# Moving a product behind stores, a load ahead of a fetch, and dealing a vector engine's rows anew, in a kernel of RWKV-7 attention and a SoLU layer

## The chip, the cores and the metric

The kernel runs on one core of a Trainium2 chip. The metric is device time in microseconds of one execution, and the median of several executions is compared. The core has five engines that run their own instruction streams in order and meet at semaphores: PE (TensorE, matrix products and transposes into the PSUM banks), DVE (VectorE), ACT (ScalarE), POOL (GpSimd) and SP (SyncE, which here only issues DMAs). POOL and ACT issue DMAs too.

## What is computed

The first part is a linear recurrence. For each of 4 batches and 8 heads a 40 x 40 state is carried over 768 steps; y is read before the state is updated. The second part takes y as 3072 rows of 320 numbers through a layer with 1024 hidden units.

```python
for t in range(S):
    y[:, :, t] = einsum('bhd,bhde->bhe', r_t, state)
    Sa = einsum('bhde,bhe->bhd', state, a_t)
    state = state * w_t[:, :, None, :] - einsum('bhd,bhe->bhde', Sa, b_t) + einsum('bhd,bhe->bhde', v_t, k_t)
x = y.transpose(0, 2, 1, 3).reshape(B * S, H * D)
h = x @ w_in
sm = softmax(h)                                  # over the 1024 hidden units
solu = h * sm
ln = (solu - mean(solu)) / sqrt(var(solu) + 1e-6) * g_ln
out = ln @ w_out
```

w_in and w_out arrive as 64-bit floats, and the kernel makes 32-bit floats of them itself, mostly with integer operations.

## The kernel before

**Chunks.** 64 steps of two batches are a chunk; a tile has 128 partitions, 64 for each batch. 12 chunks in time by 2 pairs of batches give 24 chunks, numbered 0 to 23, two in turn being independent of each other. Within a chunk the recurrence becomes matrix products: the decay's running sums (log of w, a product with a triangle on PE named pcum, exponentials ei and inv), a and b scaled by them (aT, bT; kb holds b and k times inv, made by POOL, L371), the matrix N of all pairs of a and b (nt, L453, "norm"), and the inverse of a triangular system that N gives.

**The inverse.** N of a chunk is stored to DRAM (four DMAs of nt_dram, L461). When two chunks are there, which make a block (GRP = 2; block n holds chunks 2n and 2n + 1), it is fetched back with another layout (blk, L470), and DVE solves all 32 systems of the block in step: 30 inverse steps, each of which adds to the columns found so far a multiple of a row of N (L486, or L494 and L497 in two halves). A first part (L480, L481) sets the tile up and belongs to step 1. After step 30 the result is stored (uu_dram, L503, SP) and brought back per chunk as tu and uh (L516, L518). tu is turned by DVE (flip, L524) and completed by PE, ACT, PE, ACT ("couple", "close"; py, wy, tu).

**Passes.** The main loop has passes i = -1 to 26. Pass i works on chunk i's solution (PE pu, then lu: masked on DVE, L422, and copied by ACT, L656), on chunk i + 1's scores (PE ps; DVE makes psi and lv out of it, L422; then PE px, which uses the bank pair of ps), on chunk i + 5's front (a and b turned on PE, aT on DVE, L405; norm, L453), on chunk i - 2's hidden layer (PE h, DVE nmax L735, ACT exp L743, DVE e L751, ACT sq L764, POOL rs L766), and on chunk i - 3's output (PE plnT L777, ACT lnT, PE po). PE's pst turns the carried state; DVE's tot, st and x (L682 to L698) end pass i's recurrence, and x goes through DRAM to the hidden layer. The kernel begins with a prologue that makes the fronts of chunks 0 to 4; -6 to -3 are its four turns and -2 its end.

**PSUM.** There are eight banks, used as four pairs named A, B, C and h. A new tile of a pair waits until the tile before it in that pair has been read. C holds in turn a front's turned tiles, pu, the shared tile of norm, couple and close (py), and pcum; h is used by the prologue's pcum, then by the hidden layer from pass 2 on.

**Orders.** The order on each engine is the program's, written out by hand. The inverse steps and the making of 32-bit weights are dealt out by a table `plans`: a row for each of -6 to 5 (the prologue's have five places between its steps, or two), and two rows, 24 and 25, for even and odd passes from 6 on. A pass from -1 on has six places: [0] after the front's aT and ahead of lu, [1] between lu and psi, [2] after the load of v, ahead of nmax, [3] after exp and ahead of tot, [4] after tot, [5] after st and x. In a row a number is so many inverse steps of the oldest open block ("o": of blocks that the pass needs finished, only), and b, s, f are the three parts of a weight tile's conversion: b two DVE operations (L192, L193), s three of ACT (L195, L196, L199 or L202), f three of DVE (L204 to L206); f also issues POOL's next weight load (L181) where one follows. There are 5 tiles of w_in and 8 of w_out.

**Queues.** SP issues the loads of w, b, a, k, v (L307), the fetches of tu and uh, the stores of the inverse, x's way back and the output. In the built program a DMA on SP also waits for the landing of the eighth before it. POOL issues, in its own order among the products of L371, N's stores, blk's fetch, loads of r and most loads of w_out (L181), and x's stores.

Around the change the program reads, in pass i with j = i + 5: `scaled(j + 1)` (b's and k's product), `norm(j)` (N and its stores), and in odd j `begin_inverse` (two memsets, blk's fetch). In the prologue's end: `bring(0)`, `bring(1)` (the fetches), then `load_keys(5, "bak")`.

Of the kernel before, what the change touches and what calls it, by code (L numbers as in the profile page):

```python
# [18 lines left out]
C = 64  # L19
# [4 lines left out]
LAG = 2  # L24
# [28 lines left out]
def kernel(  # L53
# [18 lines left out]
    nc = tc.nc  # L72
# [400 lines left out]
    def invert(n):  # L473
# [7 lines left out]
        nc.vector.memset(flat[0:C, 0::Q + 2], 1.0)  # L481
        for j in range(1, Q - 1):
            m, n_c = Q - 1 - j, (j + 1) // 2
            if n_c < 3:
                for c in range(n_c):
                    nc.vector.scalar_tensor_tensor(out=u[:, c, j + 1:Q], in0=nb[:, j, j + 1:Q], scalar=u[:, c, j:j + 1],  # L486
                                                   in1=u[:, c, j + 1:Q], op0=ALU.mult, op1=ALU.add)
            else:
                parts_ = ((0, n_c // 2), (n_c // 2, n_c))
                ts = []  # L490
                for lo, hi in parts_:
                    prod = two.tile([P, 72], FP32, tag="prod", name="prod")
                    ts.append(prod[:, 0:(hi - lo) * m].rearrange("p (c r) -> p c r", c=hi - lo))
                    nc.vector.tensor_tensor(out=ts[-1], in0=nb[:, j:j + 1, j + 1:Q].to_broadcast([P, hi - lo, m]),  # L494
                                            in1=u[:, lo:hi, j:j + 1].to_broadcast([P, hi - lo, m]), op=ALU.mult)
                for x, (lo, hi) in zip(ts, parts_):
                    nc.vector.tensor_tensor(out=u[:, lo:hi, j + 1:Q], in0=u[:, lo:hi, j + 1:Q], in1=x, op=ALU.add)  # L497
            if j < Q - 2:
                yield
# [143 lines left out]
    def solved(i):  # L643

        if not ok(i):
            return lambda: None
        d = st[i]
        t = pair("C", "pu")
        for u in in_turn(lambda p, q, g, h: (p ^ h, p)):
            p, q, g, h = u  # L650
            at, x = (2 * q + g) * W2, half(p ^ h)
            mm(t[half(p), h, at:at + W2], d["tu"][x, 4 * p + 2 * q + g, Q:], x0[x, h, 2 * q + g])
        lu = d["lu"] = two.tile([P, H, W2], FP32, tag="lu", name="lu", bufs=1)
        o, y = lu.rearrange("p (j h) c -> p h j c", h=2), t[:, :, 0:4 * W2].rearrange("p h (j d) -> p h j d", j=4)
        masked(o[:, :, :, 0:C], y[:, :, :, 0:C])
        return lambda: nc.scalar.copy(out=o[:, :, :, C:], in_=y[:, :, :, C:])  # L656

    def read(i, part):
        if not ok(i):
# [169 lines left out]
    for n in range(2):  # L829
# [4 lines left out]
    decay_turned(0)()  # L834
    plans = {
# [14 lines left out]
    }  # L850
# [42 lines left out]
    begin_inverse(1)  # L893
    scaled(2, "k")
    scaled(3, "k")
    load_keys(6, "w")
    vector(plan[1])
    decay(5)()
    logged(6)
    load_values(1)  # L900
    load_r(1)
    scaled(4, "k")
    bring(0)
    bring(1)
    load_keys(5, "bak")
    load_keys(7, "w")
    land(3, nc.sync)

# [1 line left out]
    for i in range(-1, N + LAG + 1):  # L910
# [58 lines left out]
        scores(i + 1)()  # L969
        flip(i + 1)  # L970
        run(2)
        scaled(j + 1)
        stated_r(i + 1)
        run(3)
        norm(j)
        if ok(j) and j % GRP == GRP - 1:
            begin_inverse(j // GRP)
        by_value(i + 2)
        run(4)
        if i == LAG + 1:  # L980
# [71 lines left out]
```

## Time and profile before

| what | value |
|---|---|
| time, median of three executions | 552.5 us (551.71, 552.5, 558.36) |
| the profiled execution | 558.81 us, of which span 557.0 us |
| granted clock of PE in it, mean | 0.969 |
| PE busy | 489.3 us, 88% of the span |
| DVE busy | 447.1 us, 80% |
| ACT busy | 300.7 us, 54% |
| POOL busy | 216.3 us, 39% |

The profile is of one execution, and its numbers are set against its own span. A row of a timeline gives the start, the length, the engine, the line of the program, the operation, the tile written and those read, the shape, how often, and in square brackets the idle time just before it with what released it. Rows of SP (SPq) are DMA issues. The chain of waits is followed back from the last instruction: each piece is what the next one waited for. Busy times overlap between engines, and an idle engine costs nothing where another sets the end.

### The profile page before, as it was taken

To read this page: it belongs to the slowest core of one execution; us is meant where nothing else is said; L and a number is where in the kernel's file an instruction comes from. 1 tells how busy PE (TensorE), PEld (TensorE's weight loads), DVE (VectorE), ACT (ScalarE), POOL (GpSimd) and SP (SyncE) were. 2 spreads that over 40 slices of the span, in tenths; PEclk is the share of its full clock that TensorE was granted. 3 is DMA by queue.
4 is the path that set the end of the run, shared out by engine and by line. 5 is a ranking of instruction groups with operands and counts; after the bars stand their busy time and mean duration, and the time that the engine had idled before them with its cause. 6 is when DMAs were issued, how large, how long until landed. Compare 5 with 4: busy or idle time off the path is not lost.

```text
span 557.0 us, 28207 instructions
## 1 busy us (share of the span) xinstructions
PE 489.3 (88%) x12081; PEld 401.1 (72%) x12081; DVE 447.1 (80%) x1801; ACT 300.7 (54%) x584; POOL 216.3 (39%) x368
## 2 busy tenths in 40 slices
PE   4644763878999999999999999999999999999996
PEld 3434653755788778878887887788778877787666
DVE  4598984799888998998989989989989788544432
ACT  4625473388376556565655655566555544653332
POOL 4456335264254264355435452644452502110110
PEclk9999976698999999999999999999999999999999
DMA  8997887665546666467566466566643432410120
GB/s 151 153 160 143 171 137 185 137 142 103 111 95 124 135 126 135 96 136 154 105 139 146 110 132 122 124 127 123 137 107 73 107 90 71 90 37 27 49 60 25
DMA packets 198157, 63.98 MB, mean 115 GB/s; under 512 B 170904, under 2 KB 190336, under 8 KB 198032
## 3 DMA queue, kind: packets, MB, share of 16 engines
q1 hardware_dynamic: 185296, 42.22, 39.8%
q0 software_dynamic: 10384, 19.30, 13.9%
q8 instruction: 95, 1.56, 1.2%
q10 hardware_dynamic: 2352, 0.66, 0.7%
q14 instruction: 30, 0.25, 0.1%
HBM read 47.96 MB, written 14.16 MB: 112 GB/s over the span
## 4 chain that ended last, share of the span: by engine, by line
PE 62%; DVE 13%; issue 9%; DMA 7%; ACT 3%; SPq 3%; POOL 2%; ACTq 0%; DVEq 0%; POOLq 0%
PE h L281 15%; PE po L281 14%; PE px L281 7%; PE py L281 5%; PE pyo L281 5%; PE pcum L281 3%; PE pu L281 3%; PE ps L281 2%; SPq L307 2%; DVE uu L497 2%; DVE prod L494 2%; PE plnT L777 2%; DMA raw_w<-in_w_dram 1%; PE pa L378 1%; PE psr L281 1%
## 5 line engine op out<-in xcount | busy, mean ns | idle before, releaser
L281 PE MATMUL h<-w_in,xT 64*64 64x512 f32 (+1 forms) x1164 | 123.1, 521 | 2.3 <-ACT lnT L786 1.1
L497 DVE TENSOR_TENSOR uu<-uu,prod 128x60 f32<-128x60 f32 (+21 forms) x624 | 117.0, 227 | 0.0
L281 PE MATMUL po<-w,lnT 128*128 128x160 f32 x768 | 109.3, 300 | 2.4 <-ACT x L641 1.6
L281 PEld LDWEIGHTS po<-w,lnT 128*128 128x128 f32 x768 | 105.3, 190 | 4.7 <-ACT x L641 2.8
L494 DVE TENSOR_TENSOR prod<-blk,uu 128x60 f32<-128x60 f32 (+21 forms) x624 | 107.1, 211 | 1.6
L766 POOL TENSOR_TENSOR rs<-var,mhalf 128x1 f32<-128x1 f32 x24 | 13.9, 578 | 182.7 <-ACT var L765 161.2
L461 POOL DMA_DIRECT2D nt_dram<-nt x86 | 50.8, 597 | 66.7 <-ACT nt L453 65.3
L281 PEld LDWEIGHTS h<-w_in,xT 64*64 64x64 f32 x1164 | 37.7, 134 | 22.2 <-issue 17.6
L735 DVE TENSOR_REDUCE nmax<-h 128x1 f32<-128x1024 f32 x24 | 29.3, 1220 | 23.7 <-PE h L281 23.7
L281 PE MATMUL pcum<-lw,cst 128*128 128x160 f32 x96 | 24.9, 394 | 16.2 <-ACT lw L347 16.2
L764 ACT ACTIVATE sq<-e,mu 128x1024 f32<-128x1024 f32 x24 | 26.9, 1119 | 16.6 <-DVE e L751 16.6
L307 POOL DMA_DIRECT2D raw_r<-in_r_dram x48 | 34.0, 714 | 1.2 <-issue 1.2
L751 DVE SCALAR_TENSOR_TENSOR e<-h,e 128x1024 f32<-128x1024 f32 x24 | 29.4, 1223 | 6.1 <-ACT e L743 6.1
L536 ACT ACTIVATE wy<-py,cst 128x256 f32<-128x256 f32 x24 | 11.3, 472 | 41.9 <-PE py L281 41.9
L743 ACT ACTIVATE e<-h,nmax 128x1024 f32<-128x1024 f32 x24 | 26.6, 1110 | 13.2 <-DVE nmax L735 13.1
L371 POOL TENSOR_TENSOR kb<-raw_b,inv 128x320 f32<-128x320 f32 x24 | 21.1, 878 | 31.2 <-DMA raw_b<-in_b_dram 23.9
L281 PEld LDWEIGHTS pcum<-lw,cst 128*128 128x128 f32 x96 | 17.8, 239 | 19.8 <-ACT lw L347 16.8
L281 PE MATMUL px<-st,aT 40*64 40x128 f32 x704 | 25.1, 281 | 6.0 <-DVE lv L422 5.0
L388 ACT COPY rT<-pb 104x512 f32<-104x512 f32 x24 | 14.1, 586 | 29.5 <-PE pb L378 29.5
L281 PEld LDWEIGHTS py<-aT,bT 40*64 40x64 f32 x768 | 17.0, 156 | 17.0 <-ACT lu L656 8.5
L801 DVE TENSOR_SCALAR osb<-po,rs 128x320 f32<-128x320 f32 x21 | 11.6, 551 | 21.7 <-POOL rs L766 12.9
L682 DVE TENSOR_TENSOR tot<-pyo,st 104x512 f32<-104x512 f32 (+1 forms) x44 | 23.9, 584 | 6.2 <-PE pyo L281 5.9
(145 smaller groups left out, 1099.4 us busy)
## 6 DMA issues: line engine op xcount, KB each, us to landing
xT<-x_dram SPq DMA_DIRECT2D x48, 160.0 KB, 3.6
blk<-nt_dram POOLq DMA_DIRECT2D x22, 256.0 KB, 4.0
raw_w<-in_w_dram SPq DMA_DIRECT2D x48, 80.0 KB, 3.5
a<-in_a_dram SPq DMA_DIRECT2D x48, 80.0 KB, 3.8
raw_r<-in_r_dram POOLq DMA_DIRECT2D x48, 80.0 KB, 3.4
lv<-in_v_dram SPq DMA_DIRECT2D x48, 80.0 KB, 3.1
out_dram<-osb SPq DMA_DIRECT2D x47, 80.0 KB, 2.6
raw_b<-in_b_dram SPq DMA_DIRECT2D x44, 80.0 KB, 3.6
```

Of the source, the lines that this page charges most:

```text
L281: nc.tensor.matmul(o, lhsT=lhsT, rhs=rhs, start=start, stop=stop, skip_group_check=True)
L307: queue.dma_start(out=x[half(p), :, 0:D], in_=ap[2 * bp + p, :, ci * C:(ci + 1) * C, :].rearrange("h t d -> t h d"))
L371: nc.gpsimd.tensor_tensor(out=kb[:, j:j + H, 0:D], in0=d["raw_" + n], in1=heads(d["inv"]), op=ALU.mult)
L388: nc.scalar.copy(out=o[0:W2], in_=t)
L461: queue.dma_start(out=blocks[n][e].rearrange("(a x h) s c -> a x s h c", a=GRP, x=2)[at, x], in_=nt[home:home + Q].rearrange("p h j c -> p ...
L494: nc.vector.tensor_tensor(out=ts[-1], in0=nb[:, j:j + 1, j + 1:Q].to_broadcast([P, hi - lo, m]), in1=u[:, lo:hi, j:j + 1].to_broadcast([P, ...
L497: nc.vector.tensor_tensor(out=u[:, lo:hi, j + 1:Q], in0=u[:, lo:hi, j + 1:Q], in1=x, op=ALU.add)
L682: nc.vector.tensor_tensor(out=by_b(tot)[:, :, :, part], in0=y[:, :, :, part], in1=by_b(state_of(i)[:, x])[:, :, :, 0:part.stop - part.star ...
L735: nc.vector.tensor_reduce(out=nmax, in_=d["h"], axis=AX.X, op=ALU.max, negate=True)
L743: nc.scalar.activation(out=e, in_=d["h"], func=AF.Exp, bias=d["nmax"], accum_out=d["esum"])
L751: nc.vector.scalar_tensor_tensor(out=d["e"], in0=d["h"], scalar=1.0 / DFF, in1=d["e"], op0=ALU.mult, op1=ALU.mult, accum_out=d["mu"])
L764: nc.scalar.activation(out=pair("A" if i > N - LAG - 1 else "h", "sq").rearrange("p a b -> p (a b)"), in_=d["e"], func=AF.Square, scale=-f ...
```

## The change

Seven edits.

- The fused form of an inverse step (L486) is used for three columns too, where two products and two adds were (steps 5 and 6 of every block).
- The solution tile pu of chunks 0 and 1 lies in the pair h, those of the others in C as before.
- For these two chunks ACT's copy of lu comes ahead of DVE's masked half in the program.
- b and a of chunk 5 are loaded by SP ahead of w of chunk 6, and so ahead of the inverse's store and of tu's fetch; k of chunk 5 stays behind the fetch.
- A second, redundant log of chunk 6's w in the prologue's end is gone (pass -1 takes it anyway).
- k's product (POOL) stands behind norm, N's stores and, in odd j, blk's fetch; b's stays.
- The plan's rows -5 to 5 are dealt anew; rows 24 and 25 are as they were.

```diff
         for j in range(1, Q - 1):
             m, n_c = Q - 1 - j, (j + 1) // 2
-            if n_c < 3:
+            if n_c < 4:
...
-        t = pair("C", "pu")
+        t = pair("C" if i >= LAG else "h", "pu")
...
+        copy = lambda: nc.scalar.copy(out=o[:, :, :, C:], in_=y[:, :, :, C:])
+        if i < LAG:
+            copy()
+            return lambda: masked(o[:, :, :, 0:C], y[:, :, :, 0:C])
         masked(o[:, :, :, 0:C], y[:, :, :, 0:C])
-        return lambda: nc.scalar.copy(out=o[:, :, :, C:], in_=y[:, :, :, C:])
+        return copy
...
         -6: ("", "", "", "", ""),
-        -5: ("b", "b", "", "s s", ""),
-        -4: ("f f", "1", "", "6", ""),
-        -3: ("1", "2", "", "", "19"),
-        -2: ("", "1"),
-        -1: ("b 2", "2 s f o1", "", "2", "", "17"),
-        0: ("1", "b", "2 s f b", "s 4 o1 b", "f b s", ""),
-        1: ("2", "3 f 1 b", "s", "8 s f", "2 b f", "3 o1"),
-        2: ("b 3 s", "f s b 1", "f s b s f 3", "3 b s", "1", "1 f"),
-        3: ("f", "4", "8", "o2", "1", "2"),
-        4: ("1", "", "9", "1", "2 o2", ""),
-        5: ("5", "1", "8", "", "", "3"),
+        -5: ("", "b", "", "b", "s s"),
+        -4: ("f", "", "f", "4", "4"),
+        -3: ("", "9", "1", "", "11"),
+        -2: ("", "1 b 1"),
+        -1: ("2", "2 s f", "o1 10", "", "", "7"),
+        0: ("b", "2 s", "2 f 1 b", "2 b", "s 1 s", "f"),
+        1: ("5", "b f 2", "o1 8 s", "o1 b f", "b s f s", "3"),
+        2: ("7", "b f b s", "f s b 1 s f 3", "1 b", "s", "f"),
+        3: ("1 f", "", "o1 10 o1", "1", "1", "2"),
+        4: ("1", "2", "11", "1", "", "o1"),
+        5: ("5", "", "9", "1", "", "2"),
...
     scaled(2, "k")
     scaled(3, "k")
+    load_keys(5, "ba")
     load_keys(6, "w")
     vector(plan[1])
     decay(5)()
-    logged(6)
     load_values(1)
     load_r(1)
     scaled(4, "k")
     bring(0)
     bring(1)
-    load_keys(5, "bak")
+    load_keys(5, "k")
...
-        scaled(j + 1)
+        scaled(j + 1, "b")
         stated_r(i + 1)
         run(3)
         norm(j)
         if ok(j) and j % GRP == GRP - 1:
             begin_inverse(j // GRP)
+        scaled(j + 1, "k")
```

## The prediction

> **What bounds the kernel now.** I read the page's slices first, then busy time by stretch.
>
> ```profile
> span 557.0 us, 28207 instructions
> ...
> PE   4644763878999999999999999999999999999996
> ```
> ```profile
> 0.00:142.00 142.00, 88.26 (x1907) 72.39 (x1911) 111.59 (x475) 76.25 (x151) 65.84 (x124) 0.88 0.77 148
> 142.00:500.00 358.00, 350.06 (x9378) 289.99 (x9374) 314.43 (x1295) 205.56 (x398) 144.64 (x234) 1.00 0.54 113
> 134.00:142.00 8.00, 7.47 (x164) 5.80 (x164) 6.48 (x16) 4.57 (x9) 5.78 (x8) 0.57 0.56 122
> ```
>
> After the length come the busy times of PE, PE's loads, DVE, ACT and POOL, then the granted clock and the DMA share. From 142 to 500 us PE idles 358 - 350.06 = 7.9 us: that stage is bound by TensorE, and only instructions taken from PE would shorten it. The diff takes none; PE's order is the same. Before 142 PE idles 142 - 88.26 = 53.7 us: the first five passes wait for other things. So the question is how much earlier the PE-bound stage begins. I follow the chain of waits back from there. It runs through block 2 of the inverse (chunks 4 and 5):
>
> ```profile
> 66.53 5.32 DMA w<-in_moe_w_in_dram
> ...
> 75.31 2.76 DMA raw_k<-in_k_dram
> ...
> 85.76 5.76 DMA blk<-nt_dram
> ```
>
> Timelines of POOL, DVE, ACT and PE around it (start, length, [idle before, releaser]):
>
> ```profile
> 76.41 0.87 POOL L371 TENSOR_TENSOR kb<-raw_b,inv 128x320 f32<-128x320 f32 x1 [8.24 <-DMA raw_b<-in_b_dram]
> 78.20 0.86 POOL L371 TENSOR_TENSOR kb<-raw_k,inv 128x320 f32<-128x320 f32 x1 [0.92 <-DMA raw_k<-in_k_dram]
> 79.00 2.33 POOL L461 DMA_DIRECT2D nt_dram<-nt  x4
> ...
> 85.23 1.07 POOL L470 DMA_DIRECT2D blk<-nt_dram  x2 [3.10 <-DMA nt_dram<-nt]
> ```
> ```profile
> 91.62 0.53 DVE L486 SCALAR_TENSOR_TENSOR uu<-blk,uu 128x30 f32<-128x30 f32 x2 [1.59 <-DMA blk<-nt_dram]
> ...
> 92.67 0.71 DVE L486 SCALAR_TENSOR_TENSOR uu<-blk,uu 128x28 f32<-128x28 f32 x4
> 93.30 0.33 DVE L494 TENSOR_TENSOR prod<-blk,uu 128x26 f32<-128x26 f32 x2
> ...
> 93.79 0.48 DVE L204 SCALAR_TENSOR_TENSOR bits<-bits,scale 128x320 int32<-128x320 int32 x1
> ...
> 96.19 0.67 DVE L422 TENSOR_TENSOR psi<-ps,cst 128x512 f32<-128x512 f32 x1
> ```
> ```profile
> 46.03 0.47 ACT L347 ACTIVATE lw<-raw_w 128x320 f32<-128x320 f32 x1 [3.11 <-DMA raw_w<-in_w_dram]
> ...
> 69.50 0.60 ACT L453 ACTIVATE nt<-py 128x512 f32<-128x512 f32 x1 [0.81 <-PE py L281]
> ...
> 92.79 0.42 ACT L656 COPY lu<-pu 128x320 f32<-128x320 f32 x1 [8.15 <-DVE lu L422]
> ```
> ```profile
> 50.68 1.08 PE L281 MATMUL py<-aT,bT 40*64 40x64 f32 x32
> ...
> 93.27 1.14 PE L281 MATMUL py<-aT,bT 40*64 40x64 f32 x32 [5.74 <-ACT lu L656]
> 97.61 1.98 PE L281 MATMUL px<-st,aT 40*64 40x128 f32 x32 [3.21 <-DVE lv L422]
> ```
>
> Chunk 5's N exists at 69.50 + 0.60 = 70.1, yet its stores start at 79.00: POOL waits first 8.24 for raw_b and then 0.92 for raw_k of chunk 6. The block lands at 91.6, DVE needs until 97.5 to free the bank of px (psi, then lv at its heels), and PE (5.74, 3.21) and ACT (8.15) stand behind DVE.
>
> **The change, part by part.**
>
> *Loads.* SP's own timeline:
>
> ```profile
> 42.56 1.30 SPq L307 DMA_DIRECT2D raw_w<-in_w_dram  x2
> 45.40 1.32 SPq L503 DMA_DIRECT2D uu_dram<-uu  x2
> ...
> 55.58 1.30 SPq L307 DMA_DIRECT2D raw_b<-in_b_dram  x2
> ...
> 60.06 1.27 SPq L307 DMA_DIRECT2D raw_k<-in_k_dram  x2
> ...
> 70.80 1.66 SPq L307 DMA_DIRECT2D raw_b<-in_b_dram  x2
> ```
>
> The four issues of b and a of chunk 5 leave the stretch 55.58 to 60.06 (4.48 us) and go ahead of raw_w at 42.56. There SP idles 1.54 us (43.86 to 45.40); two loads at 1.30 put the block-0 store at 42.56 + 3.90 = 46.46, 1.06 late, and tu's fetch with it. Net 3.4 us for all that follows, chunk 6's raw_b (70.80) among it. But ahead of that load SP also waits for landings (5.32 us in the chain). Ends 0 (landings decide) and 4.5; I take **2.5**, between the middle and the 3.4.
>
> *k behind the stores.* raw_b's product ends at 77.28, the stores start at 79.00; without k between (0.92 waiting, 0.86 working) they start when it ends: **1.7**. Queued behind the moved k are POOL's next weight load, chunk 0's x stores and raw_r, each 0.86 later against the block's fetch, but still earlier than now by more than 3; k itself is read five passes on. Block 2 then lets DVE start at 91.62 - 4.2 = 87.4.
>
> *Three-column steps.* Two products and two adds last 93.79 - 93.30 = 0.49; three fused ones, at 0.63 / 4 = 0.157 each from the 92.67 row, 0.47. Over 24 steps 0.5 us of DVE, mostly under PE: 0.
>
> *h bank, copy first, no second log.* Norm of chunk 6 no longer waits for lu (5.74), nor ACT for DVE (8.15). But both then meet px, which waits on past them (3.21) for DVE's lv: 0 on the path. If that cover goes, the 1.14 us of py would show. The second log held ACT for 3.11 us at 46; pass -1's evictions come earlier by up to that, and meet the next step:
>
> *Pass -1.* A block-1 step now stands ahead of chunk 4's aT on DVE, so behind block 1's landing:
>
> ```profile
> 47.02 0.69 DVE L405 TENSOR_TENSOR aT<-pb,ex 104x512 f32<-104x512 f32 x1 [1.65 <-ACT rT L388]
> ...
> 48.59 1.04 DVE L480 TENSOR_TENSOR uu<-blk,above 64x512 f32<-64x512 f32 x1 [0.22 <-DMA blk<-nt_dram]
> ```
>
> aT would follow at 48.59 + 1.04 and one fused step, about 49.9, and end at 50.6; its norm stands at 50.68 on PE already: 0. The four issues now ahead of raw_w, of chunk 1's v and of block 1's transfer can hold these 2.6 us at most, and the late store adds no more than its 1.06 to tu. Passes -1 and 0 are then 0 to 3.7 late, at a guess 1. Chunk 5's N, ready at 70.1, is wanted at 77.28 - 2.5 = 74.8: 4.7 of cover, so 0.
>
> *Rows.* What is left is DVE's order on the path. A plan's number is a count of inverse steps at 0.49:
>
> ```profile
> 106.35 1.02 DVE L685 COPY tot<-pyo 104x832 f32<-104x832 f32 x1 [2.89 <-PE pyo L281]
> ...
> 118.75 2.16 DVE L497 TENSOR_TENSOR uu<-uu,prod 128x48 f32<-128x48 f32 x2
> ...
> 133.51 0.68 DVE L480 TENSOR_TENSOR uu<-blk,above 64x512 f32<-64x512 f32 x1
> ```
> ```profile
> 119.03 0.87 POOL L371 TENSOR_TENSOR kb<-raw_b,inv 128x320 f32<-128x320 f32 x1
> ```
> ```profile
> 122.25 1.10 PE L281 MATMUL px<-st,aT 40*64 40x128 f32 x32 [1.21 <-DVE lv L422]
> ...
> 133.78 0.71 PE L777 MATMUL plnT<-cst,e 64*128 64x64 f32 x16 [1.97 <-ACT sq L764]
> ...
> 136.60 0.67 PE L378 MATMUL pst<-cst,st 64*104 64x64 f32 x8 [0.53 <-DVE aT L405]
> ```
>
> - Pass 1, block to psi: seven steps for six: **-0.5**. A product of POOL (119.03, k's behind it) stretches steps, whose operands all lie in SBUF: two adds take 2.16 at 118.75, where two take about 0.25 of the 0.49 at 93.30; 0.96 a product. psi, from PSUM, keeps its 0.67. Chunk 7's b product now follows the weight part that ends just before psi's last steps: ends 0 and -0.9, taken **-0.4**.
> - Pass 1, tot to chunk 7's aT: two steps fewer: **+1.0**. The steps before tot are covered by its wait of 2.89 for PE.
> - Pass 2, aT to px: three more steps (-1.5); chunk 8's b product stands behind a weight load that waits for the part finished right before psi, and k's behind the stores, so no stretch there (2.16 - 0.25 = +1.9): **+0.4**; -1.5 if stretched all the same.
> - Pass 2, px to the weighing of e: five steps for seven, small ones, two at about 0.4: **+0.8**; -0.2 if k's product stretches one of them. sq, and plnT behind it, follow.
> - Pass 3: block 3's first step (133.51, to be followed by a fused one) leaves the place ahead of aT, so pst's 0.53 goes: **+0.5**; at the low end 0.
>
> Rows 3 to 5 lie in the PE-bound stage, with the same step totals by each block's end: 0; the cover is PE's own work, and two steps ahead of psi in pass 4 would cost 1.0 without it.
>
> Sum: 2.5 + 1.7 - 0.5 - 0.4 + 1.0 + 0.4 + 0.8 + 0.5 = **6.0 us**. The profiled execution took 558.81 (span 557.0 and 1.8 around it): 552.8 by this sum. It lies 6.3 over the median of 552.5; the sum is a difference, so I take it from the median: **546.5**. With all low ends 0 + 1.7 - 0.5 - 0.9 + 1.0 - 1.5 - 0.2 + 0 = -0.4: 552.9; with all high ones 4.5 + 1.7 - 0.5 + 0 + 1.0 + 0.4 + 0.8 + 0.5 = 8.4: 544.1.
>
> **Rivals.**
>
> 1. *Landings decide, and steps stay stretched.* For it: DMA share 0.77 up to 142. Against: SP idles at 43.86. Against the stretch: POOL's new order. Without the 2.5 the gain is 3.5, with all low ends -0.4; midway **551**.
>
> 2. *PE's clock.* The stretch 134 to 142 runs at 0.57; at 1.00 its 7.47 us would be 4.3, 3.2 less: **543**; a warmer pass 1 besides, 540. Against: the 1.97 us wait before plnT remains. The Trainium skill ("TensorE: Matmul & The Clock Gate", Part 1) has the half clock begin after an idle window of about 3.4 us. By that rule a 1.97 us gap alone should not cool PE, and the stretch would go if the wait before it only shrank a little; here the slow stretch did follow a gap of 1.97, so the trace does not bear the rule out, and I keep its result as this rival.
>
> 3. *Slower: k's product in the PE-bound stage.* It moves from before lu to behind the stores, among the steps ahead of nmax, in every pass:
>
> ```profile
> 205.01 2.34 POOL L461 DMA_DIRECT2D nt_dram<-nt  x4 [4.12 <-ACT nt L453]
> ```
> ```profile
> 208.46 1.22 DVE L735 TENSOR_REDUCE nmax<-h 128x1 f32<-128x1024 f32 x1
> ```
> ```profile
> 211.02 1.11 ACT L743 ACTIVATE e<-h,nmax 128x1024 f32<-128x1024 f32 x1
> ```
>
> It would start at 207.35, every second pass later still, behind the block's fetch. A stretch of 0.96 delays nmax's end from 209.68 to 210.64; exp starts at 211.02, so 0.4 us is left. If passes are tighter by more than that, up to 0.96 over some 19 passes is 18 us; at 0.7 a pass 13.3 less the 6.0: **560**. Against: the stretch leaves the place ahead of psi, which is as near to the path.
>
> 4. *Not what it says.* The step ahead of chunk 4's aT waits so long for block 1 that passes -1 and 0 set the pace in place of chunk 6's raw_b. Against: block 1 was 0.22 late at 48.59. Beyond the 4.7 us of cover each further us costs one; at 10.7 late nothing is won: **552.5**.
>
> **How the numbers follow.** Forecast 0.48; rival 1 0.22, rival 2 0.14, rival 3 0.08, rival 4 0.08. Two per cent is 11 us, about what a measurement tells from no change: faster means under 541.5, slower over 563.5. Faster is the lower part of rival 2 and a little of the forecast: 0.11. Slower is the upper half of rival 3 and mishaps: 0.05. The range takes in rivals 1, 4 and most of 2, and leaves out 3: 540.5 to 553.5.
>
> **What would show it.** Stores of chunk 5's N directly behind raw_b's product; DVE's first step of block 2 near 87.4 for 91.62; no wait of norm or lu's copy on DVE in passes 0 and 1; px of chunk 2 near 94.3, of chunk 3 near 117.6, plnT near 128.3, pst of chunk 4 near 130.6; the same PE time from there. Wrong: raw_b of chunk 6 no earlier; stretched steps right before psi; nmax releasing exp pass after pass.

## The result, and the profile after

The changed kernel takes 551.32 us (median of 21 executions, 547.57 to 558.39), the kernel before 554.88 (21 executions beside them, 551.71 to 559.01). The ratio is **0.9928, 95% interval 0.9905 to 0.9951**: 4.0 us less. Measured once more with the last experiments the ratio was 0.9941 (0.9913 to 0.9969), 3.3 us. The forecast was 6.0 us less, 546.5. Of the 4.8 us between 546.5 and 551.3, 2.4 are the base (the three executions shown had their median at 552.5, the 21 at 554.88); the rest is the sum, of which 3.6 (by the medians) to 4.0 us (by the ratio) of 6.0 came.

The profiled execution took 552.88 us. Its page and its busy time by stretch:

```profile
span 551.1 us, 28175 instructions
...
PE   4634665888999999999999999999999999999996
```
```profile
0.00:142.00 142.00, 92.53 (x2071) 74.85 (x2073) 117.90 (x492) 78.43 (x156) 68.67 (x128) 0.89 0.78 154
142.00:500.00 358.00, 349.65 (x9412) 293.12 (x9408) 305.51 (x1257) 205.31 (x395) 143.76 (x230) 1.00 0.53 112
134.00:142.00 8.00, 7.82 (x211) 5.01 (x202) 7.96 (x30) 3.05 (x7) 3.86 (x6) 1.00 0.69 151
```

PE idles 49.5 us ahead of 142 (53.7 before) and 8.4 us in the stage bound by TensorE (7.9 before): what changed lies ahead of that stage, as argued. The granted clock from 134 to 142 is 1.00 where it was 0.57.

The same steps as before, on SP, POOL, DVE and PE:

```profile
42.57 1.30 SPq L307 DMA_DIRECT2D raw_b<-in_b_dram  x2
...
46.73 2.48 SPq L503 DMA_DIRECT2D uu_dram<-uu  x2
...
54.56 0.32 SPq L516 DMA_DIRECT2D tu<-uu_dram  x1
...
70.98 1.29 SPq L307 DMA_DIRECT2D raw_b<-in_b_dram  x2
```
```profile
74.91 1.25 POOL L371 TENSOR_TENSOR kb<-raw_b,inv 128x320 f32<-128x320 f32 x1 [10.20 <-DMA raw_b<-in_b_dram]
76.10 2.33 POOL L461 DMA_DIRECT2D nt_dram<-nt  x4
...
81.04 1.07 POOL L470 DMA_DIRECT2D blk<-nt_dram  x2 [1.75 <-DMA nt_dram<-nt]
...
92.75 0.87 POOL L371 TENSOR_TENSOR kb<-raw_b,inv 128x320 f32<-128x320 f32 x1
```
```profile
87.64 1.76 DVE L486 SCALAR_TENSOR_TENSOR uu<-blk,uu 128x30 f32<-128x30 f32 x9 [0.52 <-DMA blk<-nt_dram]
...
92.24 1.46 DVE L494 TENSOR_TENSOR prod<-blk,uu 128x48 f32<-128x48 f32 x2
...
93.86 0.68 DVE L422 TENSOR_TENSOR psi<-ps,cst 128x512 f32<-128x512 f32 x1
...
104.03 1.02 DVE L689 COPY tot<-pyo 104x832 f32<-104x832 f32 x1 [1.61 <-PE pyo L281]
```
```profile
95.29 1.99 PE L281 MATMUL px<-st,aT 40*64 40x128 f32 x32 [4.82 <-DVE lv L422]
...
129.51 0.72 PE L781 MATMUL plnT<-cst,e 64*128 64x64 f32 x16 [1.43 <-ACT sq L768]
...
131.38 0.43 PE L378 MATMUL pst<-cst,st 64*104 64x64 f32 x8 [0.26 <-DVE aT L405]
```

The stores follow raw_b's product directly, the block's first step is at 87.64 (87.4 forecast, 91.62 before), plnT at 129.51 (128.3), pst at 131.38 (130.6, 136.60 before). By these rows the sum holds almost: 5.2 us at pst. But the profiled execution of before was a late one, 3.9 us above its median; this one lies 1.6 above. A second execution of the kernel before, without any edit, says how late:

> The kernel before, unchanged, once more, for the spread of single executions. By the theory that the profiled execution of before was late in its clock alone (558.81 us against a median of 552.5 to 557): ratio 0.997 to 1.003, granted clock from 100 to 142 us above 0.83, chunk 4's pst earlier than 136.60. By the theory that the stretch belongs to the kernel: clock again near 0.83 and pst near 136.6.

Ratio 0.9992 (0.9965 to 1.0019), span of the profiled execution 551.7 us for 557.0. Its POOL, and its DVE and PE:

```profile
76.00 1.03 POOL L371 TENSOR_TENSOR kb<-raw_b,inv 128x320 f32<-128x320 f32 x1 [8.40 <-DMA raw_b<-in_b_dram]
78.55 0.88 POOL L371 TENSOR_TENSOR kb<-raw_k,inv 128x320 f32<-128x320 f32 x1 [1.52 <-DMA raw_k<-in_k_dram]
79.38 2.35 POOL L461 DMA_DIRECT2D nt_dram<-nt  x4
...
85.85 1.07 POOL L470 DMA_DIRECT2D blk<-nt_dram  x2 [3.38 <-DMA nt_dram<-nt]
```
```profile
90.51 0.53 DVE L486 SCALAR_TENSOR_TENSOR uu<-blk,uu 128x30 f32<-128x30 f32 x2 [0.30 <-DMA blk<-nt_dram]
...
95.09 0.67 DVE L422 TENSOR_TENSOR psi<-ps,cst 128x512 f32<-128x512 f32 x1
...
103.25 1.03 DVE L685 COPY tot<-pyo 104x832 f32<-104x832 f32 x1 [0.89 <-PE pyo L281]
```
```profile
96.51 1.98 PE L281 MATMUL px<-st,aT 40*64 40x128 f32 x32 [3.65 <-DVE lv L422]
...
130.73 0.72 PE L777 MATMUL plnT<-cst,e 64*128 64x64 f32 x16 [1.56 <-ACT sq L764]
...
133.55 0.43 PE L378 MATMUL pst<-cst,st 64*104 64x64 f32 x8 [1.21 <-DVE aT L405]
```

Here pst is at 133.55, three us ahead of the first execution of the same program, and the clock from 134 to 142 is 1.00. Against this one the changed kernel wins 2.2 us at pst, not 5.2. So single positions don't settle the sum. Lengths of segments do, because most repeat to a few hundredths where no landing and no clock enters; px of chunk 2 to tot and px to plnT do not (8.74 and 6.74 in the kernel before, 11.41 and 12.47 in the changed one), and are read as averages. The table gives starts and segments (us) from the timelines of all that was run; "both" below means the loads and k edits together. In p1_all psi comes ahead of the block, so its "to psi" is negative.

| execution | stores of chunk 5's N | block 2's first step | to psi | px of chunk 2 to tot | tot to aT of 7 | aT to px of 3 | px to plnT | plnT to pst | pst to px of 4 | px of chunk 4 |
|---|---|---|---|---|---|---|---|---|---|---|
| before | 79.00 | 91.62 | 4.57 | 8.74 | 6.72 | 9.18 | 11.53 | 2.82 | 9.70 | 146.30 |
| before, once more | 79.38 | 90.51 | 4.58 | 6.74 | 6.72 | 9.20 | 11.56 | 2.82 | 7.50 | 141.05 |
| bank_only | 77.57 | 89.60 | 4.57 | 8.74 | 6.72 | 9.18 | 11.54 | 2.82 | 7.96 | 142.55 |
| loads_only | 77.38 | 90.45 | 4.57 | 8.74 | 6.71 | 9.19 | 11.53 | 2.82 | 7.49 | 142.92 |
| k_only | 76.92 | 87.74 | 5.55 | 8.52 | 6.73 | 8.39 | 11.99 | 2.82 | 7.49 | 140.65 |
| k_first_passes | 77.21 | 89.40 | 5.54 | 8.74 | 6.71 | 8.38 | 12.29 | 2.82 | 9.74 | 145.04 |
| rows_only | 77.34 | 90.96 | 5.23 | 6.96 | 5.53 | 8.55 | 12.47 | 1.86 | 8.06 | 141.05 |
| rows_back | 75.93 | 87.96 | 4.48 | 8.34 | 7.11 | 9.00 | 12.25 | 2.82 | 9.95 | 143.34 |
| k_back | 78.29 | 90.04 | 5.09 | 6.96 | 5.53 | 8.55 | 11.95 | 1.86 | 8.06 | 139.47 |
| loads_back | 76.19 | 88.93 | 6.21 | 8.74 | 5.53 | 8.55 | 12.46 | 1.85 | 8.00 | 141.70 |
| bank_back | 73.96 | 85.12 | 6.22 | 8.73 | 5.53 | 8.57 | 12.48 | 1.86 | 7.63 | 137.57 |
| fused_back | 75.61 | 86.96 | 6.36 | 7.06 | 5.53 | 8.55 | 12.23 | 1.86 | 8.00 | 137.98 |
| step_behind | 75.76 | 87.14 | 6.21 | 8.74 | 5.52 | 8.55 | 11.69 | 1.86 | 7.63 | 138.77 |
| changed | 76.10 | 87.64 | 6.22 | 8.74 | 5.53 | 8.54 | 11.41 | 1.87 | 8.02 | 139.40 |
| changed, once more | 74.95 | 86.26 | 6.22 | 8.73 | 5.53 | 8.55 | 12.47 | 1.85 | 8.02 | 139.06 |
| k_early | 75.38 | 86.95 | 6.22 | 7.66 | 5.52 | 8.56 | 11.95 | 1.86 | 7.99 | 138.13 |
| b6_early | 71.59 | 86.41 | 6.22 | 8.73 | 5.53 | 8.55 | 11.96 | 1.86 | 8.01 | 138.70 |
| p1_two | 75.19 | 87.01 | 4.13 | 9.39 | 5.51 | 8.57 | 11.96 | 1.85 | 8.00 | 137.85 |
| p1_all | 74.49 | 96.77 | -7.43 | 14.91 | 6.05 | 8.56 | 11.69 | 1.85 | 7.63 | 141.46 |
| combined | 71.93 | 84.60 | 4.36 | 11.72 | 5.52 | 8.67 | 12.23 | 1.85 | 8.00 | 138.38 |

### The profile page after: what moved, and what is told of

Its sections match the earlier page's. It is cut to its first block, busy times and chain, and to the rows that moved or that the text cites. A ratio compares the mean times of both kernels' runs of the same rounds, so it can differ in the third digit from the quotient of the medians.

```text
span 551.1 us, 28175 instructions
## 1 busy us (share of the span) xinstructions
PE 487.2 (88%) x12081; PEld 402.7 (73%) x12081; DVE 442.2 (80%) x1777; ACT 300.7 (55%) x583; POOL 218.2 (40%) x368
## 3 DMA queue, kind: packets, MB, share of 16 engines
q8 instruction: 95, 1.56, 1.2%
## 4 chain that ended last, share of the span: by engine, by line
PE 53%; DVE 17%; issue 11%; DMA 8%; ACT 5%; SPq 3%; POOL 3%; ACTq 0%; POOLq 0%; DVEq 0%
PE h L281 13%; PE po L281 12%; PE px L281 5%; PE py L281 5%; PE pyo L281 4%; DVE prod L494 3%; DVE uu L497 3%; PE pu L281 2%; PE ps L281 2%; PE pcum L281 2%; DVE uu L486 2%; DMA raw_w<-in_w_dram 2%; SPq L307 2%; PE plnT L781 2%; DMA uu_dram<-uu 1%
## 5 line engine op out<-in xcount | busy, mean ns | idle before, releaser
L281 PE MATMUL h<-w_in,xT 64*64 64x512 f32 (+1 forms) x1164 | 124.5, 518 | 1.3 <-ACT lnT L790 1.1
L494 DVE TENSOR_TENSOR prod<-blk,uu 128x48 f32<-128x48 f32 (+19 forms) x576 | 107.7, 227 | 1.3
L497 DVE TENSOR_TENSOR uu<-uu,prod 128x48 f32<-128x48 f32 (+19 forms) x576 | 98.2, 210 | 0.0
L461 POOL DMA_DIRECT2D nt_dram<-nt x86 | 50.7, 597 | 75.4 <-ACT nt L453 74.0
L281 PEld LDWEIGHTS h<-w_in,xT 64*64 64x64 f32 x1164 | 40.7, 133 | 20.5 <-issue 16.5
L536 ACT ACTIVATE wy<-py,cst 128x256 f32<-128x256 f32 x24 | 11.4, 474 | 44.0 <-PE py L281 44.0
L486 DVE SCALAR_TENSOR_TENSOR uu<-blk,uu 128x30 f32<-128x30 f32 (+3 forms) x144 | 29.9, 263 | 2.9 <-DMA blk<-nt_dram 2.0
L595 ACT COPY st<-psr 128x512 f32<-128x512 f32 x22 | 12.9, 585 | 35.5 <-PE psr L281 35.4
L281 PEld LDWEIGHTS py<-tu,nt 64*64 64x64 f32 x768 | 18.9, 143 | 16.2 <-issue 9.5
L422 DVE TENSOR_TENSOR lu<-pu,cst 128x512 f32<-128x512 f32 x24 | 16.5, 687 | 16.8 <-PE pu L281 16.5
```

The lines of the kernel that those rows point to most:

```text
L281: nc.tensor.matmul(o, lhsT=lhsT, rhs=rhs, start=start, stop=stop, skip_group_check=True)
L422: nc.vector.tensor_tensor(out=dst, in0=t, in1=tri.unsqueeze(1).unsqueeze(1).to_broadcast([P, 2, 4, C]), op=ALU.mult)
L461: queue.dma_start(out=blocks[n][e].rearrange("(a x h) s c -> a x s h c", a=GRP, x=2)[at, x], in_=nt[home:home + Q].rearrange("p h j c -> p ...
```

## Experiments

Ratios are against the kernel before on the same chip, with intervals of 0.2 to 0.35% to either side, 1 to 2 us. Two neighbouring ratios differ surely only where they are some 0.4% apart.

**Each edit alone.**

```diff
-        scaled(j + 1)
+        scaled(j + 1, "b")
...
             begin_inverse(j // GRP)
+        scaled(j + 1, "k")
```

> The kernel before with one edit: k's product behind norm, N's stores and blk's fetch. By the prediction's term: N's stores of chunk 5 start right behind raw_b's product, block 2 reaches DVE 1.7 us earlier (about 89.9 for 91.62), and the time is 1.7 us lower, ratio 0.997. By the theory that the whole gain of the change came from POOL's order: 3 to 4 us lower, ratio 0.993 to 0.995. By the theory that steps ahead of psi, now stretched by POOL, take it back: under 0.5 us, ratio above 0.999.

1.0002 (0.9972 to 1.0031). The stores follow raw_b's product, the block comes at 87.74; but POOL's product now meets DVE's work ahead of psi, and the segment grows from 4.57 to 5.55. Nothing is left in the time: the third theory's number. The stretch by itself takes 1.0 of the 2.8 to 3.9 us by which the block is earlier; the rest of why nothing is left is not shown, and the interval is 1.6 us to either side.

```diff
+    load_keys(5, "ba")
     load_keys(6, "w")
...
-    load_keys(5, "bak")
+    load_keys(5, "k")
```

> The kernel before with one edit: b and a of chunk 5 are loaded ahead of w of chunk 6 and of the inverse's store. By the prediction's term: raw_b of chunk 6 is issued 2.5 us earlier (about 68.3 for 70.80), ratio 0.9955. By the theory that SP's issue of that load is set by landings and that the inverse's store and tu's fetch lose what the loads leave: issue within 0.5 us of 70.8, ratio between 0.999 and 1.003, and tu's fetch about 3.5 us late (54.5 for 51.03).

1.0012 (0.9982 to 1.0042). Its POOL shows why:

```profile
74.38 0.87 POOL L371 TENSOR_TENSOR kb<-raw_b,inv 128x320 f32<-128x320 f32 x1 [6.71 <-DMA raw_b<-in_b_dram]
76.58 0.86 POOL L371 TENSOR_TENSOR kb<-raw_k,inv 128x320 f32<-128x320 f32 x1 [1.33 <-DMA raw_k<-in_k_dram]
```

raw_b's product is 1.6 to 2.0 us earlier than in the two executions of before, and then the stores wait 1.33 for raw_k and 0.86 for its product, and start at 77.38. SP issues raw_b at 68.94 (1.6 to 1.9 earlier) and tu's fetch at 53.87 (2.6 to 2.8 later).

```diff
-        1: ("2", "3 f 1 b", "s", "8 s f", "2 b f", "3 o1"),
+        1: ("5", "b f 2", "o1 8 s", "o1 b f", "b s f s", "3"),
...
```

> The kernel before with one edit: the plan's rows -5 to 5 as in the changed kernel. By the prediction's terms -0.5 - 0.4 + 1.0 + 0.4 + 0.8 + 0.5: 1.8 us lower, ratio 0.9967; the gains lie between tot of pass 1 and pst of chunk 4. By the theory that the rows gave most of the change: 3 us or more, ratio 0.9945 or less. By the theory that they only gave back what the earlier block won: no gain, ratio 0.999 to 1.002.

0.9966 (0.9933 to 0.9999), 1.9 us, as forecast for the rows, though not by the forecast's terms (below).

```diff
-        t = pair("C", "pu")
+        t = pair("C" if i >= LAG else "h", "pu")
...
+        if i < LAG:
+            copy()
+            return lambda: masked(o[:, :, :, 0:C], y[:, :, :, 0:C])
```

> The kernel before with one edit: pu of chunks 0 and 1 in pair h, lu copied, then masked. By the prediction: norm of chunk 6 starts some 4 us earlier, px of chunk 2 does not, ratio 0.999 to 1.001. By the theory that undoing it in the changed kernel showed its true worth (0.9975 against 0.9928): 0.994 to 0.997.

1.0002 (0.9983 to 1.0021). Norm of chunk 6 (py) starts 4.4 to 5.5 us earlier than in the two of before, and px waits for lv behind it, 6.74 us for 3.21 and 3.65; px itself is earlier only by as much as the block happened to be (first step 89.60 for 91.62 and 90.51):

```profile
87.77 1.08 PE L281 MATMUL py<-aT,bT 40*64 40x64 f32 x32
95.59 1.98 PE L281 MATMUL px<-st,aT 40*64 40x128 f32 x32 [6.74 <-DVE lv L422]
```

**Each edit undone in the changed kernel** (the diffs are the ones above, reversed; the last has one of its own).

> The changed kernel with k's product put back ahead of norm and the stores. By the prediction's term the time is 1.7 us above the changed kernel's, 0.9958 of the kernel before if the changed one is at 0.9928. By the theory that the whole gain came from POOL's order: 0.998 to 1.0. By the theory that the order of POOL does nothing in the end: 0.993, and N's stores of chunk 5 about 1.8 us later, but px of chunk 3 no later.

0.9959 (0.9928 to 0.9991). The stores start at 78.29, behind raw_k, and to psi it takes 5.09 for 6.22.

> The changed kernel with b and a of chunk 5 loaded behind tu's fetch again. By the prediction's term: raw_b of chunk 6 is issued 2.5 us later, and the time is 0.9973 of the kernel before (0.9928 of the change, and 2.5 us). By the theory that the loads give nothing on the path, because passes -1 and 0 grow late by as much: 0.991 to 0.995, tu's fetch near 51, couple of chunk 0 (PE, py) back near 55 from 58.3, and the product of chunk 6's b no later than 75.5.

0.9982 (0.9952 to 1.0012); couple of chunk 0 is at 58.51, no earlier than the changed kernel's 58.28, because the step ahead of chunk 4's aT still waits for block 1 (5.77 us). That expectation of the second theory failed. So did the first theory's later issue: SP issues chunk 6's raw_b at 71.02, for 70.98 and 69.36 in the changed kernel's two executions, though the ratio is near the first theory's 0.9973.

> The changed kernel with pu of chunks 0 and 1 in pair C again and lu masked first. By the prediction (the waits of norm and lu only pass on to the wait of px for lv): norm of chunk 6 waits some 5 us for lu again, px of chunk 2 starts where it does in the changed kernel, 95.3, and the time is 0.991 to 0.995. By the theory that these waits were the part of the gain that no other edit shows: 0.996 or more, px of chunk 2 later by over 1 us.

0.9975 (0.995 to 0.9999). Yet px of chunk 2 is not later (92.77), and norm waits for nothing: the five steps ahead of lu start at 85.12 here, and lu's copy ends in time. Neither theory's picture; the ratio has no row behind it.

> The changed kernel with the plan's rows -5 to 5 of the kernel before. By the prediction's terms for the rows (1.8 us): 0.996 of the kernel before. By the theory that the other edits only pay with the new rows, as the edit of k alone and the loads alone (ratios 1.000 and 1.001) suggest: 0.998 to 1.001.

0.9987 (0.9957 to 1.0016): without the new rows the rest gives 0.7 us, which is not clear of none. That is the second theory's number, and the interval just takes in the first theory's 0.996.

```diff
-            if n_c < 4:
+            if n_c < 3:
```

> The changed kernel with two products and two adds for three columns again (steps 5 and 6 of every block). By the prediction's term (0.5 us of DVE over 24 steps, under PE): 0.991 to 0.995, and steps ahead of psi in pass 1 the same within 0.1 us but for what POOL stretches. By the theory that fused steps are what POOL's product stretches less: psi of pass 1 0.5 to 1 us later against the block's first step, 0.994 to 0.996.

0.9978 (0.9944 to 1.0013), psi 6.36 behind the block's first step for 6.22. Again the row is as forecast, and the ratio is above it.

The five undone edits cost 1.7 to 3.3 us each against 0.9928, 13 us together, over three times the whole gain. So the changed kernel was run once more, unedited:

> The changed kernel, unchanged, once more, beside the runs that vary it. If its first ratio is its true one: 0.991 to 0.995. If undoing one edit cost 1.7 to 3.3 us in every run because the first comparison came out low by chance: 0.995 to 0.997, and the sum of the undone parts shrinks by the same.

0.9941 (0.9913 to 0.9969), within the first theory's range, but 0.7 us above the first measurement. The kernel's ratio is near 0.9935. The segments show what loads and k do to the block, and that the pair does more than either alone (numbers below). In the time the pair by itself is not clear of none (rows_back); the rows alone just are (0.9966). What the other undone edits are worth is not resolved: executions of one program differ by more than that: from tot of pass 3 to tot of pass 20 the first profiled execution of the changed kernel took 321.22 us, the second 323.90.

**The PE-bound stage** (rival 3). Two kernels have k's later place in passes -1 to 4 alone:

```diff
+        scaled(j + 1, "b" if i < 5 else "bk")
...
+        if i < 5:
+            scaled(j + 1, "k")
```

> The kernel before with k's product behind the stores in passes -1 to 4 alone; from pass 5 on it stands ahead of norm again. By the theory that the later place costs in the PE-bound stage (about 0.2 us a pass, what the one profile of the edit alone shows from pass 4 to 17) and gains 3 to 4 us ahead of it: 0.993 to 0.995 of the kernel before, and tot of pass 20 still 3 us earlier than before's. By the theory that the place costs nothing there and that the earlier block is eaten elsewhere: the same as with the edit in all passes, 0.998 to 1.002.

> The changed kernel with k's product back ahead of norm from pass 5 on, and behind the stores before that. By the theory that the later place costs in the PE-bound stage: 0.987 to 0.991 of the kernel before, 1 to 3 us below the changed kernel. By the theory that it costs nothing there: 0.991 to 0.995, like the changed kernel.

1.0019 (0.9992 to 1.0046) for the first, 0.9926 (0.99 to 0.9952) for the second, on the changed kernel: no gain from putting k back. The collision is real, though. Pass 11 of the changed kernel, then of k_early, on DVE:

```profile
292.22 0.43 DVE L524 STREAM_TRANSPOSE tu<-tu 128x256 f32<-128x256 f32 x1
...
296.19 1.02 DVE L497 TENSOR_TENSOR uu<-uu,prod 128x60 f32<-128x60 f32 x2
297.13 1.00 DVE L494 TENSOR_TENSOR prod<-blk,uu 128x57 f32<-128x57 f32 x2
...
298.85 1.21 DVE L739 TENSOR_REDUCE nmax<-h 128x1 f32<-128x1024 f32 x1
```
```profile
290.80 0.43 DVE L524 STREAM_TRANSPOSE tu<-tu 128x256 f32<-128x256 f32 x1
...
296.07 1.22 DVE L739 TENSOR_REDUCE nmax<-h 128x1 f32<-128x1024 f32 x1
```

nmax comes 6.6 us behind flip for 5.3; two steps are stretched by 0.66 each. But passes 11 and 12 together last 37.9 us in the one (19.65 + 18.29) and 37.8 in the other (18.93 + 18.84): what the odd pass loses the even one gives back.

**What comes next behind the block.** One more load earlier:

```diff
         if i == -1:
+            load_keys(6, "b")
             load_values(2)
...
-        load_keys(j + 2, "bak")
+        load_keys(j + 2, "bak" if i >= 0 else "ak")
```

> The changed kernel with one more load moved: b of chunk 6 is loaded ahead of v of chunk 2 and of the two weight loads of pass -1, so about 8 us earlier (near 62.5 for 70.98). By the prediction's step, that chunk 6's b holds N's stores and the block behind it: its product ends ahead of N of chunk 5 (71.7), the stores start near 72.5 for 76.10, block 2 reaches DVE 3 to 3.6 us earlier, and with what lies behind it paying about one for one the time is 0.986 to 0.988 of the kernel before. By the theory that landings ahead of the block's fetch, or the stage behind it, take it back: 0.991 to 0.995.

0.9923 (0.9899 to 0.9946). Its POOL:

```profile
67.63 0.87 POOL L371 TENSOR_TENSOR kb<-raw_b,inv 128x320 f32<-128x320 f32 x1 [3.05 <-ACT kvT L562]
71.59 2.33 POOL L461 DMA_DIRECT2D nt_dram<-nt  x4 [3.09 <-ACT nt L453]
...
78.52 1.07 POOL L470 DMA_DIRECT2D blk<-nt_dram  x2 [3.86 <-DMA nt_dram<-nt]
```

The stores start 3.4 to 4.5 us earlier, now right behind N itself. But from the stores to the block's fetch it takes 6.9 us for 4.9 and 5.2, and the first step is at 86.41, inside the changed kernel's two (86.26, 87.64). The landings took it.

Fewer steps ahead of psi in pass 1:

```diff
-        1: ("5", "b f 2", "o1 8 s", "o1 b f", "b s f s", "3"),
+        1: ("5", "b f", "o1 10 s", "o1 b f", "b s f s", "3"),
```

> The changed kernel with two inverse steps of pass 1 taken from ahead of psi to behind it (row 1 of the plan: 5 and 0 in place of 5 and 2 ahead of psi, 10 in place of 8 ahead of tot). By the theory that the two steps that POOL's product stretches (0.55 and 1.78 us at 91.78 and 92.24) hold PE at px of chunk 2: psi 2 us earlier against the block's first step (4.2 us behind it for 6.22), tot of pass 1 1.5 to 2 us earlier, 0.989 to 0.990 of the kernel before. By the theory that DVE as a whole bounds this stretch, so that steps put behind psi only hold tot instead: tot no more than 0.7 us earlier, 0.992 to 0.994.

0.9956 (0.993 to 0.9982). psi comes 4.13 behind the first step, 2.1 us won; tot takes 0.7 of them back (9.39 for 8.74) and lies at 101.96 right behind DVE's own work. Up to there the first theory's number (2.1 and 0.7 ahead of the changed kernel's two), in the time none of it.

```diff
-        1: ("5", "b f 2", "o1 8 s", "o1 b f", "b s f s", "3"),
+        1: ("", "b f", "o1 15 s", "o1 b f", "b s f s", "3"),
```

> The changed kernel with all seven inverse steps of pass 1 that stand ahead of psi taken behind it (0 and 0 ahead of psi, 15 ahead of tot), so that psi does not wait for the block at all. By the theory that the block holds PE only through the steps put ahead of psi: psi near 89 for 93.86, tot of pass 1 2.5 to 3 us earlier, 0.987 to 0.989 of the kernel before. By the theory that DVE as a whole is the bound from the block's landing on: psi as early, but tot no more than 1 us earlier and released by DVE's own steps, 0.991 to 0.993.

1.0004 (0.9973 to 1.0035). psi is at 89.34 as the first theory has it, but flip, next on DVE, waits for tu's fetch, and the block waits behind flip:

```profile
95.63 0.45 DVE L524 STREAM_TRANSPOSE tu<-tu 128x256 f32<-128x256 f32 x1 [5.01 <-DMA tu<-uu_dram]
```

tot comes at 105.68, later than the changed kernel's. Neither theory had this wait.

```diff
-        -2: ("", "1 b 1"),
-        -1: ("2", "2 s f", "o1 10", "", "", "7"),
+        -2: ("", "1 b"),
+        -1: ("3", "2 s f", "o1 10", "", "", "7"),
```

> The changed kernel with the step of block 1 that stands ahead of chunk 4's aT put behind it (row -2 ends after b, row -1 begins with 3 for 2). By the prediction (passes -1 and 0 late by 0 to 3.7 us, under a cover of 4.7): aT of chunk 4 some 3 to 4 us earlier (near 48 for 51.89), nothing from block 2 on, 0.991 to 0.995. By the theory that the cover is gone: 0.987 to 0.990.

0.9963 (0.9934 to 0.9993); aT of chunk 4 is at 46.02 for 51.89, block 2's first step at 87.14. Nothing won: the cover held.

> The changed kernel with three of the tried edits: chunk 6's b loaded ahead of pass -1's weights, two steps of pass 1 behind psi, k's product behind the stores up to pass 4 only. Adding what the profiles showed up to tot of pass 3 (0.7, 1.5) and the 1 to 1.5 us that the PE-bound stage was longer with the later place: 3 to 4 us below the changed kernel measured beside it, 0.986 to 0.990. By the theory that each of them ends in the same next wait (flip behind tu's fetch, tot behind DVE's own steps): no more than 1 us below it.

0.9957 (0.9933 to 0.9981). px of chunk 2 comes at 90.39, 3.5 to 4.9 us ahead of the changed kernel's two, and 0.7 to 1.0 us of it is left at px of chunk 4 (138.38). It is the three edits above in one: b of chunk 6 earlier, two steps behind psi, k late up to pass 4. flip waits again, 4.31 us:

```profile
94.55 0.45 DVE L524 STREAM_TRANSPOSE tu<-tu 128x256 f32<-128x256 f32 x1 [4.31 <-DMA tu<-uu_dram]
```

No version beat the changed kernel by more than the intervals.

## Why the prediction was right or wrong

The sign held, and so did the frame: the stage from 142 us on stayed bound by TensorE (PE idles 8.4 us in it, 7.9 before), and the gain lies ahead of it. The size was off, and one step failed in its mechanism: the way from px of chunk 3 to plnT, which the prediction put on DVE's steps. It put that at +0.8 us, and the rows have -0.6. The base was off as well: 552.5, from three executions, for 554.88. Term by term, with what the segments measured (starts are means over the profiled executions that have an edit; they scatter by about 1 us):

- **Loads, +2.5: measured 1.3.** raw_b's product starts at 74.2 on average in eleven executions with the loads moved as in the changed kernel and at 75.5 in seven without, and SP issues the load only 0.7 us earlier (69.9 for 70.6). What left the stretch behind tu's fetch came back ahead of it: the store's issue took 2.48 us for 1.32 (1.98 to 4.42 in the eleven, 1.32 or 1.33 in the seven), and the fetch was 3.5 us late where 1.06 was put. This is rival 1's "landings decide", by half; b6_early, where the landings took 3.4 to 4.5 us, shows it whole.
- **k behind the stores, +1.7: measured 2.1**, about what the wait and the work of raw_k's product said (from the start of raw_b's product to the stores 3.1 us on average in the six executions without the edit, 1.0 in the twelve with it; b6_early and combined, where the stores wait for N, are left out). What the sum missed is that the two terms are no plain sum. The stores start at 78.3 with neither edit; with the loads alone (two executions) they still wait for raw_k and start at 77.8; with k alone (three) at 76.8; with both (eight; p1_all, where the block waits behind flip, is left out) at 75.4. The block's first step is at 90.7 with neither (four), 90.3 with the loads alone, 88.7 with k alone and 86.9 with both: 3.8 for the 4.2 of the sum, of which 3.0 are there when the stores start.
- **Three columns 0, bank and copy 0:** as the rows say (6.36 for 6.22; px waits 6.74 in place of 5.74 and 3.21). The ratios of undoing them (0.9978, 0.9975) are above the changed kernel's, with nothing in the rows to account for it; that stays open. The second log was not run by itself.
- **Pass -1, 0:** pass -1 came 0.5 to 2 us late (chunk 4's norm at 52.63 and 52.08 for 50.68 and 51.56), inside the range given; chunk 5's norm did not (68.97 and 69.08 for 68.74 and 70.01); the cover held, and step_behind shows nothing behind it. Rival 4 falls.
- **Pass 1, seven steps for six, -0.5: measured -0.5** (k_back: 5.09 for 4.57).
- **Pass 1, POOL's stretch, -0.4: measured -1.1**, beyond its low end of -0.9. chunk 7's b product starts at 92.75, and the product at 92.24 takes 1.46 for the 0.33 it takes in k_back. The two ends "0" and "0.9" were the two ways the step could fall; it was not halfway but fully hit, in every execution with the new row of pass 1 and k's later place (loads_back too, 6.21). With the old row it is not (rows_back, 4.48).
- **Pass 1, tot to aT, +1.0: measured 1.2; pass 2, aT to px, +0.4: measured 0.6.** Both held.
- **Pass 2, px to the weighing of e, +0.8: measured about -0.6** (px to plnT 12.1 on average, 11.4 to 12.5, in the 13 executions with the new rows, for 11.5 in the four with the old rows and k's old place). This step failed in its mechanism. "sq, and plnT behind it, follow" the weighing is how it was before, but only by 0.20 us. ACT and DVE before, then ACT and DVE of the changed kernel:

```profile
128.45 1.11 ACT L743 ACTIVATE e<-h,nmax 128x1024 f32<-128x1024 f32 x1
...
132.49 1.12 ACT L764 ACTIVATE sq<-e,mu 128x1024 f32<-128x1024 f32 x1 [0.20 <-DVE e L751]
```
```profile
131.23 1.22 DVE L751 SCALAR_TENSOR_TENSOR e<-h,e 128x1024 f32<-128x1024 f32 x1
```
```profile
123.95 0.86 ACT L641 ACTIVATE x<-px 128x832 f32<-128x832 f32 x1 [0.37 <-PE px L281]
124.71 1.11 ACT L747 ACTIVATE e<-h,nmax 128x1024 f32<-128x1024 f32 x1
...
128.22 1.11 ACT L768 ACTIVATE sq<-e,mu 128x1024 f32<-128x1024 f32 x1
```
```profile
124.31 0.92 DVE L494 TENSOR_TENSOR prod<-blk,uu 128x7 f32<-128x7 f32 x2
...
126.82 1.22 DVE L755 SCALAR_TENSOR_TENSOR e<-h,e 128x1024 f32<-128x1024 f32 x1
```

Before, the weighing ends at 132.45 and sq starts 0.04 later, 4.04 behind exp. In the changed kernel the weighing starts 8.72 us behind px for 8.98, so 0.3 of the 0.8 came: k's product stretches the product at 124.31 (0.92 for 0.24 before), as the low end of -0.2 had it. But sq no longer waits for DVE: it starts 0.18 us behind the weighing's end (0.18 to 1.06 in all 13) and 3.51 us behind exp (3.51 or 3.52 in all 13), by what ACT has queued between them. Steps taken from DVE could win 0.20 us here, and from there ACT's queue decides. exp in its turn stands behind ACT's x, behind PE's px and close, and it comes 6.61 us behind px of chunk 3 in this execution and up to 7.69 in the others, for 6.20 and 6.63 in the two of before. Where it comes later, the segment is longer. In two of the 13 (rows_only and the second execution of the changed kernel) px of chunk 3 runs at half clock (1.95 and 1.99 us for 1.10). In the other 11 close starts 0.4 to 1.5 us behind the end of wy, for 0.06 and 0.4 in the two of before; the rows put part of this down to wy, which has ended by then; what close waits for they do not show, and that stays open.
- **Pass 3, +0.5: measured 0.95** to pst (2.82 less 1.86); then 0.5 is lost from pst to px of chunk 4 (8.0 for 7.5).

With these sizes the sum is 3.8 - 0.5 - 1.1 + 1.2 + 0.6 - 0.6 + 0.95 - 0.5 = **3.85 us** for 6.0, and 4.0 and 3.3 were measured. The largest misses are the way from px to the weighing and plnT (1.4), the stretch (0.7) and loads with k (0.4). px of chunk 2 to tot is left out of this sum, because it goes with the clock of the single execution (last section).

**Rival 2** was given 0.14 and came in part: the slow stretch went, but the time is not near its 543. With the old rows plnT waits 1.56 to 2.01 us for sq, and in four of seven profiled executions a stretch below full clock follows, which makes pst to px 7.96 to 9.95 us for 7.5; with the new rows the wait is 1.42 or 1.43 in all 13, and the clock is 1.00 in all. One of the four, k_first_passes:

```profile
130.00:134.00 4.00, 1.99 (x56) 1.84 (x54) 3.92 (x12) 3.76 (x10) 1.17 (x2) 0.91 0.47 71
134.00:138.00 4.00, 3.37 (x38) 1.82 (x38) 3.85 (x6) 2.84 (x5) 3.55 (x6) 0.50 0.55 115
```

So the rival's condition, a wait a little shorter, came with the new rows. The Trainium skill ("TensorE: Matmul & The Clock Gate", Part 1) has the half clock begin after an idle window of about 3.4 us, free-running; here the half clock followed a wait of 1.97 to 2.01 us in four of five executions, and one of 1.58 or less in none of 15. PE's work around the wait is sparse too (1.99 of 4 us busy in the first row), so that the wait alone does it is not shown. Where that gain went in the time isn't settled: it should be worth 1 us on average (2.4 at the most), and 3.3 to 4.0 is what the sum gives without it. The later place of k may cost as much in the PE-bound stage: passes 3 to 20 take 323.4 us on average in 11 executions that have it there and 322.3 in nine that don't, a difference no larger than the scatter of single executions (1.2 us, standard deviation), and the timed pairs don't show it.

**Rival 3** fell as a price: the collision is there in odd passes, and the next pass makes it up. **Rival 1** named two things that the rows show: landings took half of the loads' term, and steps ahead of psi stayed stretched. That 551 is also the measured time is luck: it stood for 1.5 us less than 552.5, and the gain was 3.3 to 4.0 us from a base of 554.9.

## What to carry to other kernels

When a store waits for two loads in turn, hastening the first does little while the second is still waited for (0.5 us at the stores here, 3.0 with both edits); work out the pair, and try it as a pair. Before counting work removed from an engine as a gain, read how far ahead it is of the next thing that the same step needs: here DVE held sq by 0.20 us, and then ACT's queue did. And take a second profiled execution of the kernel before: position differences of 3 us lay between two executions of one program, while most segment lengths repeated to 0.02 us and carried the account.

## What the runs showed of the hardware

- One POOL product of two SBUF tiles (0.87 us) lengthens what DVE runs beside it by 0.65 to 1.1 us, not only steps with two tiles from SBUF: in k_only and k_first_passes the weight operation L193, which reads one, took 1.36 us for 0.32. psi and lv, which read PSUM, kept their 0.67 to 0.69. The Trainium skill ("SBUF — State Buffer", Who interferes with whom) names the port pair that the two engines share, for instructions with two SBUF inputs and for those in a two-port mode; the first agrees with the rows, and whether L193 ran in such a mode no run here shows.
- The time from px of chunk 2 to tot is 8.7 us in most executions and 6.7 to 7.1 in four, by the granted clock (the column before the DMA share). The second execution of before, then the changed kernel:

```profile
98.00:101.00 3.00, 2.46 (x76) 2.35 (x68) 2.97 (x23) 0.46 (x1) 1.13 (x2) 0.65 0.78 172
101.00:104.00 3.00, 2.94 (x101) 2.76 (x102) 2.08 (x4) 1.81 (x5) 0.59 (x1) 1.00 0.70 107
```
```profile
98.00:101.00 3.00, 2.40 (x84) 2.27 (x80) 2.97 (x22) 0.47 (x1) 0.00 (x0) 0.50 0.64 106
101.00:104.00 3.00, 3.00 (x73) 2.76 (x67) 1.39 (x4) 1.69 (x4) 0.62 (x1) 0.53 0.69 112
```

PE is at half clock when px starts (96.51 and 95.29) and busy from there but for one pause of 0.60 us. In the one it is at full clock some 3.5 us later, in the other some 8.5. These 2 us come and go with the execution, in the kernel before itself (8.74 and 6.74), and are half of what the change is worth.
